# A second routing round held back in the list of the first expert's work, and its steps listed closer together

## The chip, the cores and the metric

The kernel runs on one core of one Trainium2 chip. Its time is the device time of one launch in microseconds (us), the median of several runs. A core has five engines with a queue each, and each queue is worked off in the order in which the program lists it: TensorE (PE, matrix products), VectorE (DVE), ScalarE (ACT), GpSimd (POOL) and SyncE (SP, which here only issues transfers).

## What is computed

The reference chains three blocks over 4608 tokens of width 512. Retention attention makes x. A dense block with 2048 hidden units follows, and then a block of eight experts with 1024 hidden units each, in which every expert gets exactly 576 tokens:

```
x = retention(q, k, v)                    # 4608 x 512
x = (h - tanh(h)) @ w_out,  h = x @ w_in
logits = x @ w_gate                       # 4608 x 8
pairs (token, expert) in falling order of logit: take a pair if the token is
still free and the expert has fewer than 576 tokens
out[tokens of e] = relu(x[tokens of e] @ w1[e]) @ w2[e]
```

Products have single-precision accuracy: each operand is split into a high and a low part, and three products (high-high, high-low, low-high) are added.

## The kernel before

Attention and the dense block take the first 1017 us of the profiled execution and are not touched. What follows is `phase_c`: routing and experts.

**Routing** is done in eight rounds (`route(r)`). A round settles which expert is filled next (`EI[r]`, line 990) and which 576 tokens it gets (`IDX[r]`, line 1050). A round is one long chain that goes to and fro between VectorE and TensorE: proposals (lines 857 to 863, the mask `P`), then six threshold steps, each with a comparison (`cmp`, lines 839, 908, 925), nine or eighteen small matmuls that count (930 or 934), a scaling `ca` (938), small matmuls (949, 950) and a search (957 to 960); then `GG` (969), matmuls 973 and 975, the choice of the expert (979 to 990), matmuls 995 and 996, positions (999 to 1018), `R` on ScalarE (1019), `A` and `R` on VectorE (1021, 1023), matmuls 1027 and 1045, and the list of tokens.

**An expert** (`experts(r)`) runs 192 matmuls of its first layer (line 1158, eight blocks f of 24) and 112 of its second (line 1189, five token tiles in the order 0, 4, 1, 2, 3). After each block of the first layer ScalarE makes `hh` (1167) and a split weight `w2h` (1074), GpSimd makes `w2l` (1075), and VectorE makes the low part `hl` (1171), which is listed six matmuls into the next block. The PSUM pool `psF` has four buffers of which a block takes two, so block f+2 waits until `hl` of block f is made.

**The next expert's needs** are prepared meanwhile: eight weight tiles are loaded by SP (1063) as soon as `EI` is known, split by ScalarE (`w1h`) and GpSimd (`w1l`, both 1074/1075); five token tiles are gathered by GpSimd (`xg`, 1097) from the list of tokens, turned by TensorE (`tp`, 1112, two buffers), copied by ScalarE (`xh`, 1114) and subtracted by VectorE (`xl`, 1115).

**The order in each queue** is set by three generators, `threads`: 0 for routing, 1 for weights, 2 for tokens. Each `yield d` says how many units later the next step may be listed. The expert loop calls `tick` as it lists matmuls (0.24 units for two of the first layer, 0.213 for one of the second); a thread whose time has come lists its next step there. For routing d is scaled by `YS[0]` while only the first round's token list exists and by `YS[1]` after that; for weights and tokens it is scaled by `YS[0]` throughout. No number of these is a time on the chip; they only place instructions.

Before expert 0 the first round runs alone. Then 14 matmuls keep TensorE busy (1215) while the first tokens are gathered, and the second round (r = 1) and the turning of the five token tiles are listed into one another until expert 0 starts. The second round then goes on inside expert 0, the third inside expert 1, and so on; the last two rounds end inside expert 5.

Of the kernel before, what the change touches and what calls it, by code (L numbers as in the profile page):

```python
# [125 lines left out]
@with_exitstack  # L126
def moe_kernel(ctx, tc, qkv, wio, wgt, wgk, ident, w1, w2, qtab, vtab, amask, cint, rtf, rti, rth, rtb, out):
    nc = tc.nc
    ctx.enter_context(tc.manual_schedule())
    cpool = ctx.enter_context(tc.tile_pool(name="cpool", bufs=1))  # L130
    dpool = ctx.enter_context(tc.tile_pool(name="dpool", bufs=1, space=DRAM))
    x2d = dpool.tile([NTOK, DM], F32, name="x2d")
    L = cpool.tile([128, NCOL, E], F32, name="L")

    with ExitStack() as bs:
        phase_ab(tc, bs, qkv, wio, wgt, wgk, ident, qtab, vtab, amask, cint, x2d, L)
    with ExitStack() as cs:
        phase_c(tc, cs, w1, w2, rtf, rti, rth, rtb, x2d, L, out)
# [594 lines left out]

Y_TR, Y_CA, Y_H, Y_GG, Y_X, Y_Z, Y_R, Y_IX = 2.0, 0.85, 0.5, 2.9, 2.7, 4.2, 1.8, 2.7

YS = 0.82, 0.85
TK1 = 0.24
TK2 = 0.213

# [9 lines left out]
def phase_c(tc, ctx, w1, w2, rtf, rti, rth, rtb, x2d, L, out):  # L749
# [369 lines left out]
    def each(f):  # L1119
        for r in range(E):  # L1120
            for d in f(r):
                yield d

    threads = [[0.0, each(f)] for f in (route, weights, tokens)]
    clock = [0.0]

    def tick(dt):
        clock[0] += dt
        for th_ in threads:
            while th_[1] is not None and th_[0] <= clock[0]:  # L1130
# [3 lines left out]
                else:  # L1134
                    th_[0] = clock[0] + d * (YS[len(IDX) > 1] if th_ is threads[0] else YS[0])

# [77 lines left out]
    for _ in range(WARM2):  # L1214
        nc.tensor.matmul(warm, B["ones"], tb[:, 256:768], start=True, stop=True)

    threads[2][0] = 2.0
    while 0 not in XT:
        tick(0.2)
    for r in range(E):  # L1220
# [83 lines left out]
```

## Time and profile before

| | |
|---|---|
| median of 3 runs | 1554.09 us (1553.83 to 1555.44) |
| profiled execution, its own time | 1556.99 us |
| its span, first to last instruction | 1555.1 us |
| TensorE busy | 1456.5 us, 94% of the span |
| VectorE, ScalarE, GpSimd busy | 73%, 49%, 36% |
| mean granted TensorE clock | 0.973 of full speed |
| expert 0, first matmul | 1070.40 us into the span |

Times in the rows below are us from the span's start. The profiled execution has 1.9 us around its span, and lies 2.9 us above the median of the runs; differences are worked out within its span and then put on the median.

### The profile page before, as it was taken

The numbers are of one execution on the slowest core, as the hardware profiler recorded it, in microseconds if no ns is written. First come the engines' busy times: TensorE is split into PE (matmuls) and PEld (weight loads), VectorE is DVE, ScalarE is ACT, GpSimd is POOL, SyncE is SP. The second block draws the span as 40 slices with busy tenths as digits, with TensorE's granted clock in tenths as the row PEclk, the third lists the DMA queues.
The fourth block names the chain that finished last, engine by engine and source line by source line (L and its number), as shares of the span: only waits on it lengthen the run. The fifth ranks groups of instructions, "written<-read, shape, count | busy, mean of one in ns | idle before, by whom it ended". The sixth has DMA issues, their size and how long they took to land.

```text
span 1555.1 us, 26174 instructions
## 1 busy us (share of the span) xinstructions
PE 1456.5 (94%) x9500; PEld 1276.3 (82%) x9500; DVE 1132.7 (73%) x2740; ACT 761.5 (49%) x1585; POOL 558.3 (36%) x492
## 2 busy tenths in 40 slices
PE   5989899899999999999999999937999999999997
PEld 4777788789898989898989898825788887887996
DVE  7999965878787878777878787867776766765210
ACT  4767775455656565656564646503333323323421
POOL 4546541212222221212121223224535535446541
PEclk7999999999999999999999999967999999999999
DMA  7522222111111111111111100013423423426210
GB/s 258 197 72 82 82 104 74 43 62 42 62 41 62 42 62 42 62 41 62 42 54 50 43 22 21 1 37 129 125 85 124 129 85 120 130 84 193 91 65 31
DMA packets 48610, 122.43 MB, mean 79 GB/s; under 512 B 6624, under 2 KB 13408, under 8 KB 48224
## 3 DMA queue, kind: packets, MB, share of 16 engines
q1 hardware_dynamic: 41184, 99.80, 19.2%
q0 software_dynamic: 6144, 19.93, 4.0%
q8 instruction: 75, 1.23, 0.3%
q10 hardware_dynamic: 1152, 1.02, 0.2%
q14 instruction: 55, 0.45, 0.1%
HBM read 101.85 MB, written 18.87 MB: 78 GB/s over the span
## 4 chain that ended last, share of the span: by engine, by line
PE 73%; DVE 14%; issue 4%; ACT 3%; POOL 2%; DMA 1%; SPq 0%; POOLq 0%; DVEq 0%; ACTq 0%
PE h L426 22%; PE x L489 21%; PE ff L1189 11%; PE ff L1158 10%; PE pb L290 2%; PE pb L357 2%; PE pb L369 1%; DVE work L208 1%; DVE t L456 1%; DVE t L450 1%; DVE junk L530 1%; DVE t L452 1%; PE tp L1112 1%; PE pb L305 1%; DVE h L454 1%
## 5 line engine op out<-in xcount | busy, mean ns | idle before, releaser
L470 POOL TENSOR_TENSOR gl<-t,gh 128x384 fp32r<-128x384 f32 x192 | 200.2, 1043 | 652.6 <-ACT gh L467 565.8
L426 PE MATMUL h<-xh,w0h 128*128 128x384 f32 x704 | 240.4, 341 | 11.8 <-DVE t L456 11.6
L426 PE MATMUL h<-xh,w0l 128*128 128x384 f32 x704 | 238.3, 338 | 0.0
L436 ACT ACTIVATE S<-h 128x384 f32<-128x384 f32 x192 | 93.7, 488 | 286.7 <-PE h L426 286.5
L489 PE MATMUL x<-w1h,gh 128*128 128x512 f32 x576 | 231.2, 401 | 0.5 <-ACT gh L467 0.5
L489 PE MATMUL x<-w1l,gh 128*128 128x512 f32 x576 | 226.9, 394 | 0.0
L489 PE MATMUL x<-w1h,gl 128*128 128x512 f32 x576 | 217.0, 395 | 1.3 <-POOL gl L470 1.0
L450 DVE SCALAR_TENSOR_TENSOR t<-t,S 128x384 f32<-128x384 f32 x192 | 114.1, 594 | 128.7 <-ACT t L439 128.1
L530 DVE SCALAR_TENSOR_TENSOR junk<-x2r,wg 128x512 f32<-128x512 f32 x240 | 168.7, 703 | 5.2
L426 PE MATMUL h<-xl,w0h 128*128 128x384 f32 x704 | 152.6, 338 | 0.0
L426 PEld LDWEIGHTS h<-xh,w0h 128*128 128x128 f32 x704 | 132.7, 188 | 23.4 <-DVE t L456 12.3
L1075 POOL TENSOR_TENSOR w2l<-ws,w2h 128x512 fp32r<-128x512 f32 x64 | 82.6, 1293 | 161.4 <-ACT w2h L1074 161.4
L426 PEld LDWEIGHTS h<-xh,w0l 128*128 128x128 f32 x704 | 133.1, 189 | 6.7
L489 PEld LDWEIGHTS x<-w1h,gl 128*128 128x128 f32 x576 | 108.1, 188 | 29.7 <-POOL gl L470 5.7
L1189 PE MATMUL ff<-w2h,hh 128*128 128x512 f32 x320 | 127.5, 399 | 3.1 <-DVE hl L1171 2.0
L456 DVE COPY_PREDICATED t<-m,h 128x384 f32<-128x384 uint16 x192 | 114.4, 596 | 20.9 <-ACT m L445 1.7
L1189 PE MATMUL ff<-w2l,hh 128*128 128x512 f32 (+1 forms) x320 | 127.4, 398 | 0.6 <-POOL w2l L1075 0.6
L489 PEld LDWEIGHTS x<-w1h,gh 128*128 128x128 f32 x576 | 108.6, 188 | 22.9 <-ACT gh L467 1.3
L426 PEld LDWEIGHTS h<-xl,w0h 128*128 128x128 f32 x704 | 126.7, 189 | 0.3 <-DVE xl L413 0.2
L439 ACT ACTIVATE t<-S,bias 128x384 f32<-128x384 f32 x192 | 118.3, 616 | 17.4 <-POOL gl L470 0.9
L489 PEld LDWEIGHTS x<-w1l,gh 128*128 128x128 f32 x576 | 108.6, 189 | 17.1
L1158 PE MATMUL ff<-xh,w1h 128*128 128x288 f32 x512 | 115.0, 302 | 6.3 <-DVE hl L1171 5.5
(212 smaller groups left out, 2989.6 us busy)
## 6 DMA issues: line engine op xcount, KB each, us to landing
ws<-in_w SPq DMA_DIRECT2D x128, 256.0 KB, 2.8
ain<-in_qkv SPq DMA_DIRECT2D x36, 768.0 KB, 4.2
wst<-in_wio SPq DMA_DIRECT2D x32, 512.0 KB, 3.5
x2d<-x2r SPq DMA_DIRECT2D x33, 256.0 KB, 2.0
w1h<-in_qkv SPq DMA_DIRECT2D x12, 192.0 KB, 4.6
w1l<-in_qkv SPq DMA_DIRECT2D x12, 192.0 KB, 3.5
w0h<-in_qkv SPq DMA_DIRECT2D x12, 192.0 KB, 4.0
w0l<-in_qkv SPq DMA_DIRECT2D x12, 192.0 KB, 4.1
```

Of the source, the lines that this page charges most:

```text
L290: nc.tensor.matmul(PSA[k][a][:, chunk(c)], kt[r, chunk(c)], q[r, chunk(c)], start=True, stop=True)
L426: nc.tensor.matmul(h[:, :TB], w[0][f][:, hp, :], x, start=i == 0, stop=i == 11)
L436: nc.scalar.activation(S, h, AF.Square, scale=KSC)
L439: nc.scalar.activation(AT[s][2], AT[s][1], AF.Square, bias=bias[:, 0:1])
L450: nc.vector.scalar_tensor_tensor(t, t, PA - PB * PB / 4, S, op0=OP.add, op1=OP.mult)
L456: nc.vector.copy_predicated(t, m.bitcast(U16), h)
L470: nc.gpsimd.tensor_tensor(G[s][1], TT.pop(s), G[s][0].bitcast(F32), op=OP.subtract)
L489: nc.tensor.matmul(X2[n][i], g[:, i * 128:i * 128 + 128], w, start=(f == 0 and g is gh and w is wh), stop=(f == NF - 1 and g is gl))
L530: nc.vector.scalar_tensor_tensor(j, r, 1.0, wg[e // 4][:, e % 4, :], op0=OP.mult, op1=OP.mult, accum_out=L[:, c, e:e + 1])
L1075: nc.gpsimd.tensor_tensor(l, s, h.bitcast(F32), op=OP.subtract)
L1158: nc.tensor.matmul(ps[u], w[:, k, :], x[:, k, 288 * u:288 * u + 288], start=i == 0, stop=i == 11)
L1189: nc.tensor.matmul(o, h, w, start=f == 0 and i == 0, stop=f == 7 and i == len(prods) - 1, skip_group_check=t == 4)
```

## The change

Two places change. The scale of the second routing round, and of all later steps of weights and tokens, goes from 0.82 to 0.75. And after the warm-up matmuls the first four steps of the second round are listed at once (its proposals on VectorE, as before), and its next step may be listed only from 7.0 units on, while the tokens' thread still starts at 2.0.

```
-YS = 0.82, 0.85
+YS = 0.75, 0.85
@@ phase_c, after the warm-up matmuls (line 1215)
-    threads[2][0] = 2.0
+    for _ in range(4):
+        next(threads[0][1])
+    threads[0][0], threads[2][0] = 7.0, 2.0
     while 0 not in XT:
         tick(0.2)
```

What this does to the queues at three places follows.

VectorE ahead of expert 0. `ca`, `cmp` and the rows from 957 on are the second round's; `xl` are the five token tiles of expert 0. Before:

```order
L938 TENSOR_TENSOR ca<-rt,tf 128x32
L1115 TENSOR_TENSOR xl_10796<-tp,xh_10795 128x4x128
L957 TENSOR_REDUCE d_10822<-rt 128x8
L958 TENSOR_REDUCE dm_10819<-d_10822 128x1
L959 STREAM_TRANSPOSE tr_10820<-dm_10819 128x32
L960 SCALAR_TENSOR_TENSOR tr_10820,pi<-tr_10820,st 128x31
L916 TENSOR_SCALAR st<-tf,pi 128x32
L925 TENSOR_TENSOR cmp_10827<-hi,st 128x1152
L1115 TENSOR_TENSOR xl_10796<-tp,xh_10795 128x4x128 x2
L938 TENSOR_TENSOR ca<-rt,tf 128x32
```

After:

```order
L1115 TENSOR_TENSOR xl_10796<-tp,xh_10795 128x4x128 x4
L938 TENSOR_TENSOR ca<-rt,tf 128x32
L1115 TENSOR_TENSOR xl_10796<-tp,xh_10795 128x4x64
L957 TENSOR_REDUCE d_10850<-rt 128x8
L958 TENSOR_REDUCE dm_10847<-d_10850 128x1
L959 STREAM_TRANSPOSE tr_10848<-dm_10847 128x32
L960 SCALAR_TENSOR_TENSOR tr_10848,pi<-tr_10848,st 128x31
L916 TENSOR_SCALAR st<-tf,pi 128x32
L925 TENSOR_TENSOR cmp_10855<-hi,st 128x1152
```

All five token tiles now stand ahead of the round's next search and comparison; the matmuls 930 that wait for that comparison move from between the third and fourth tile to behind 16 matmuls of expert 0.

ScalarE at the end of expert 0's first layer: the last block's `hh` and `w2h`, the routing's `R`, and the first split weights `w1h` of expert 1. Before:

```order
L1074 ACTIVATE w2h_11286<-ws_11121 128x512
L1019 ACTIVATE R<-b_11382,tf 128x36x20
L1167 ACTIVATE hh<-ff 128x288 x2
L1074 ACTIVATE w2h_11390<-ws_11177 128x512
L1074 ACTIVATE w1h_11399<-ws 128x512
```

After:

```order
L1074 ACTIVATE w2h_11270<-ws_11095 128x512
L1167 ACTIVATE hh<-ff 128x288 x2
L1074 ACTIVATE w2h_11323<-ws_11148 128x512
L1074 ACTIVATE w1h_11379<-ws 128x512
L1074 ACTIVATE w1h_11389<-ws 128x512
L1019 ACTIVATE R<-b_11416,tf 128x36x20
```

`R`, which waits for a long chain on VectorE, stood ahead of the last block's `hh` and now stands behind it and behind two split weights. On GpSimd, at the same place, the first gather for expert 1 stood behind seven of the eight `w1l` and now stands behind all eight.

TensorE at the end of expert 1's first layer; 995 and 996 are the third round's. Before (18 first-layer matmuls still follow these rows):

```order
L1158 MATMUL ff<-xh_11583,w1h_11517 128x288 x2
L995 LDWEIGHTS tb
L995 MATMUL rt<-X,tb 128x72
L996 LDWEIGHTS tb
L996 MATMUL rt<-X,tb 128x72
L1158 MATMUL ff<-xh_11583,w1l_11518 128x288 x2
```

After:

```order
L1158 MATMUL ff<-xl_11577,w1h_11502 128x288 x8
L995 LDWEIGHTS tb
L995 MATMUL rt<-X,tb 128x72
L996 LDWEIGHTS tb
L996 MATMUL rt<-X,tb 128x72
L1189 MATMUL ff<-w2h_11772,hh 128x512
```

The routing steps stand some 18 matmuls later within expert 1, and 995 is now the last thing ahead of the second layer, the place at which it stood in expert 0 before.

## Rows read from the trace of the kernel before

**Rows 1.** The page: engines' busy time (share) xinstructions, and the weight loads
```profile
PE 1456.5 (94%) x9500; PEld 1276.3 (82%) x9500; DVE 1132.7 (73%) x2740; ACT 761.5 (49%) x1585; POOL 558.3 (36%) x492
...
ws<-in_w SPq DMA_DIRECT2D x128, 256.0 KB, 2.8
```

**Rows 2.** Timeline, start of expert 0: start, us, engine, line, operation, count [idle before <-releaser]
```profile
1065.00 0.69 DVE L1115 TENSOR_TENSOR xl<-tp,xh 128x512 fp32r<-128x512 f32 x1 [1.15 <-ACT xh L1114]
1065.71 0.19 DVE L957 TENSOR_REDUCE d<-rt 128x8 f32<-128x32 f32 x1
...
1065.75 0.66 PE L1112 MATMUL tp<-tf,xg 128*128 128x128 f32 x4 [1.11 <-DVE xl L1115]
1065.77 1.26 ACT L1114 ACTIVATE xh<-tp 128x512 fp32r<-128x512 f32 x2 [0.81 <-PE tp L1112]
...
1066.90 1.35 DVE L925 TENSOR_TENSOR cmp<-hi,st 128x1152 bf16<-128x1152 int32 x1
...
1068.31 0.39 PE L930 MATMUL rt<-P,cmp 128*128 128x32 bf16 x9 [1.91 <-DVE cmp L925]
...
1070.40 0.59 PE L1158 MATMUL ff<-xh,w1h 128*128 128x288 f32 x1
...
1075.19 0.61 PE L934 MATMUL rt<-P,cmp 128*128 128x16 bf16 x18 [0.73 <-DVE cmp L925]
```

**Rows 3.** Windows: us; PE, PEld, DVE, ACT, POOL busy (xinstructions); granted clock, DMA share, GB/s
```profile
1066.00:1068.00 2.00, 0.40 (x4) 0.16 (x2) 1.86 (x6) 0.97 (x2) 2.00 (x3) 1.00 0.27 107
...
1070.00:1072.00 2.00, 2.00 (x11) 2.00 (x10) 1.62 (x7) 0.59 (x2) 2.00 (x2) 0.50 0.00 0
```

**Rows 4.** Timeline, TensorE in expert 0's first layer: two places of the second round
```profile
1081.25 0.39 PE L930 MATMUL rt<-P,cmp 128*128 128x32 bf16 x9
...
1097.81 0.42 PE L973 MATMUL rt<-GG,tb 128*128 128x192 bf16 x3
```

**Rows 5.** Timeline, end of expert 0's first layer: the choice of expert 1, its loads
```profile
1100.06 0.14 DVE L990 TENSOR_SCALAR ei<-mx 128x1 int32<-128x1 f32 x1
...
1101.32 5.15 SPq L1063 DMA_DIRECT2D ws<-in_w  x8
```

**Rows 6.** Timeline, ScalarE and TensorE at expert 0's second layer: R and the waits
```profile
1104.92 0.90 ACT L1019 ACTIVATE R<-b,tf 128x720 bf16<-128x720 bf16 x1 [6.35 <-DVE b L1018]
...
1106.98 0.50 PE L1189 MATMUL ff<-w2h,hh 128*128 128x512 f32 x1 [1.08 <-ACT w2h L1074]
...
1108.35 0.50 PE L1189 MATMUL ff<-w2l,hh 128*128 128x512 f32 x1 [0.63 <-POOL w2l L1075]
...
1123.05 0.66 PE L1112 MATMUL tp<-tf,xg 128*128 128x128 f32 x4 [0.68 <-DMA xg<-x2d,idx]
...
1125.47 0.66 PE L1112 MATMUL tp<-tf,xg 128*128 128x128 f32 x4 [0.36 <-DMA xg<-x2d,idx]
```

**Rows 7.** Timeline, GpSimd there: split weights of expert 1 and the first gather
```profile
1108.25 5.05 POOL L1075 TENSOR_TENSOR w1l<-ws,w1h 128x512 fp32r<-128x512 f32 x4
...
1119.67 0.97 POOL L1097 DMA_INDIRECT xg<-x2d,idx  x1 [0.30 <-DVE lo L903]
```

**Rows 8.** Waits of TensorE, 1140 to 1556 us: line waited for: total, times, longest us
```profile
PE ff L1158 <- DVE hl L1171: 5.5, 6, 2.0
PE ff L1189 <- DVE hl L1171: 2.0, 2, 1.1
PE tp L1112 <- DVE xl L1115: 1.4, 1, 1.4
```

**Rows 9.** Timeline, TensorE: the longest waits of experts 1, 3, 4 and 5
```profile
1165.62 0.50 PE L1189 MATMUL ff<-w2h,hh 128*128 128x512 f32 x1 [1.10 <-DVE hl L1171]
...
1285.96 0.89 PE L1158 MATMUL ff<-xh,w1h 128*128 128x288 f32 x2 [1.99 <-DVE hl L1171]
...
1342.67 0.89 PE L1158 MATMUL ff<-xh,w1h 128*128 128x288 f32 x2 [1.10 <-DVE hl L1171]
...
1402.81 0.89 PE L1158 MATMUL ff<-xh,w1h 128*128 128x288 f32 x2 [1.20 <-DVE hl L1171]
```

## Prediction, made before the changed kernel was run

> **What bounds the kernel now.** I read the page first. TensorE is busy for 1456.5 us of the 1555.1 us span, 94%, VectorE for 1132.7, the other two for far less [rows 1]. The change takes away no matmul and adds none, so the time can move in two ways only: TensorE's idle time at waits, and the clock at which it runs. The second view is the timeline at the start of expert 0, where the list is changed [rows 2, 3]; the reader is to see there which wait ends last before each matmul. The third is the end of expert 0, where every routing step now stands later than before [rows 4 to 7]. The fourth is the list of TensorE's waits over the later experts [rows 8, 9], since the new scale acts on all of them.
>
> At the start the turning of expert 0's tokens and the search of the second round share VectorE and TensorE. The fourth tile's `tp` waits 1.11 us for `xl`, which came behind earlier work of the round, and the nine matmuls 930 wait 1.91 us for `cmp`, with the last turn behind them [rows 2]. TensorE is busy for 0.40 us of the 2 us from 1066; its granted clock is 1.00 there, and 0.50 (1.2 GHz) from 1070 to 1072, when expert 0's matmuls have begun [rows 3].
>
> In the late experts TensorE waits mostly for `hl`: 5.5 us ahead of first-layer matmuls, 2.0 ahead of second-layer ones, plus 1.4 for one `xl` [rows 8]. Together that is 8.9 us, the largest part of what a new order can win or lose behind expert 0.
>
> **Start of expert 0.** With the round held back, `tp` depends on ScalarE and VectorE's token copies alone. Two `xh` take 1.26 us, so one takes 0.63, and one `xl` takes 0.69 [rows 2]. With two `tp` buffers the last tiles follow each other at about 1.3 us: third tile at about 1065.5, fourth 1066.8, the last (half a tile) 1068.1, and its `xl` is done by about 1068.8. `ca` follows at once. Expert 0's first matmul then comes at about 1069.0 instead of 1070.40: **1.4 us won** (1.1 to 2.1).
>
> What was held back is paid for next. The chain from 957 to the end of `cmp` runs from 1065.71 to 1066.90 + 1.35, that is 2.54 us [rows 2]. It now starts when `ca` and the last `xl` are done, about 0.8 us behind the first matmul, so `cmp` is ready 3.3 us behind it. 930 stands behind 16 matmuls; at full clock they take 16 x 0.135 = 2.2 us (112 of them with the small matmuls between take 1097.81 - 1081.25 = 16.56 us, 0.148 each [rows 4]; without the small ones I put one at 0.135). So 930 waits about 1.1 us. The next step, 934, stands 42 matmuls later (6.0 us with what lies between), and its chain of `ca`, search and two `cmp` takes about 6.7, so it waits 0.7; before it waited 0.73 [rows 2], which is no change. Low clock: the window 1070 to 1072 at half speed cost about 1.0 us [rows 3]. With shorter idle times ahead I take it as gone at this place. First matmul 1069.0, plus 60 x 0.135, plus the two waits, plus 0.9 for the small matmuls is 1079.9. Before, 930 behind 60 matmuls ran at 1081.25 [rows 4]. So **-1.35 us** after a third of the first layer (bounds -2.1, if both waits are absent, and 0, if both chains are one us longer than read).
>
> **End of expert 0.** Here the new scale does more than the hold. 973 ran behind 172 first-layer matmuls [rows 4] and now stands four matmuls into the second layer; 995 goes from the end of the first layer to 14 matmuls into the second.
>
> What goes: `R` stood ahead of the last `hh` on ScalarE, idle for 6.35 us before it. Because of this `w2h` came 1.08 us late and `w2l` 0.63 [rows 6]. With `R` behind them both waits go: **-1.7 us**.
>
> What comes: VectorE has the last `hl` ahead of the choice of the expert now, so `ei` moves from 1100.06 [rows 5] to about 1103.3. SP issued the loads 1.26 us later [rows 5]; a load takes 2.8 us [rows 1], then one `w1h`. So the first `w1l` starts at about 1107.95, hardly different from 1108.25, because before `R` had held `w1h` back too. GpSimd took 11.4 us from its first `w1l` to the first gather, with seven `w1l` and two stores between [rows 7]. Now all eight stand ahead: 5.05 / 4 = 1.26 more, and the gather starts at about 1120.7. It landed 3.38 us after it started (1119.67 to 1123.05 [rows 6, 7]), so the first turn can run at 1124.2. TensorE gets there earlier than before: the turn stands five second-layer matmuls later (b80 instead of b75), but 1.35 and 1.7 us are saved and one step of the third round has moved behind it. I work out 1120.0. So it **waits 4.2 us** where it waited 0.68 + 0.36 [rows 6]: +3.2. The other four gathers follow in 1.26 us each, the turns every 1.6, so they don't wait. Bounds: nothing, if GpSimd comes to the gather at 1116.6 or before; 5.5, if a store to `out` gets in its way by another us. I take 4.2 because every term has its own row.
>
> Sum up to the end of expert 0: -1.35 - 1.7 + 3.2 = **+0.1**. The gain of the start is spent within one expert.
>
> **Clock behind the new wait.** At the start an idle stretch was followed by 2 us at 0.50, costing 1.0 [rows 3]. A single wait of 4.2 us is longer than the idle time there. Between 0 and 1.0, I take **+0.5**, as nothing shows whether the fall comes while TensorE waits (and costs nothing) or behind it. On this the Trainium skill (TensorE: Matmul & The Clock Gate, section "HAM oscillation — how this bites in real kernels") says that a matmul loop that stops for transfers is throttled again at each stop and begins its next burst at the low clock. By that rule this term would be 1.0 and the forecast 1557.1; it speaks against this change, which trades a wait for VectorE at a place that was slow already for a wait for a gather.
>
> **Later experts.** Every routing step stands some 18 matmuls later in each expert, which is nearly what one expert shifts the round anyway. So expert k+1 of after should look like expert k of before: one more expert of the early, crowded kind. Before, experts 1 to 5 wait for 1.1 (its second layer), about 2.0, 2.6 (of which 1.99 is one wait), 1.1, and 2.6 (of which 1.20): 9.4 us [rows 8, 9]. After: expert 1 gets what expert 0 had, with 995 at the end of its first layer and `R` ahead of the last `hh`: 1.7 [rows 6], plus about 1.1 at a gather that follows; expert 2 some 1.2; expert 3 some 2.1; expert 4 the 2.0 of expert 3 and 1.1 of its own [rows 9]; expert 5 some 2.1. That is 11.3, **+1.9**. Bounds: -4 (most of the `hl` waits go, since `hl` comes to stand ahead of the searches that delay it) and +4 (each of the five experts keeps its wait and the one of its neighbour).
>
> Total: +0.1 + 0.5 + 1.9 = +2.5 us, 1559.5 by the profiled execution's own 1556.99 and 1556.6 on the median, since that execution lies 2.9 above the median. What this kernel's measurement can tell from no change is about 0.2%, 3.1 us: the forecast lies just inside.
>
> **Rivals.** *The `hl` waits go (faster).* One mechanism, in experts 2 to 5 on VectorE: `hl` waits behind a search or comparison listed ahead of it, and with the steps moved by 18 of a block's 24 matmuls it may stand ahead of them. It decides at whether VectorE can begin `hl` when `hh` is ready; if so the 7.5 us of [rows 8] shrink to 3 to 4. For it: that is the largest group of waits. Against it: the same move puts other `hl` behind other steps, as in experts 3 to 5 of before. Price: later experts -3 instead of +1.9, so about 1551.6. *All late steps lose (slower).* The gather wait costs 5, the clock a full 1.0, 1027 waits for an `R` that stands behind two `w1h`, and the later experts lose 4: +6, about 1559.8. For it: the gather stands behind all eight `w1l` on a queue of one. Against it: nothing shows that waits at neighbouring experts add. *Nothing happens.* The start's 1.4 us are eaten by 930 and 934, the turn's wait is some 2 us shorter than worked out because GpSimd's order is looser than read, and the later waits only change place: about 1554.
>
> **How the numbers follow.** Forecast 0.48, centre 1556.6, its own range 1555 to 1558.3; `hl` waits go 0.13; all lose 0.26; nothing 0.13. Slower by over 0.2% (above 1557.2) takes the second rival whole and 0.15 of the forecast: 0.41. Faster by over 0.2% (below 1551.0) takes most of the first: 0.12. Within: 0.47. The range of 1552.5 to 1560.0 leaves out about 0.1 at either end.
>
> **What would show it.** First matmul of expert 0 at about 1069.0; a wait of about 1.1 us at 930 behind 16 matmuls. No wait for `w2h` or `w2l` in expert 0, and waits of 1.08 and 0.63 us of this kind at expert 1 instead. The first gather at about 1120.7 and the first turn behind it with a wait of about 4.2 us for `xg`: this is the step on which most hangs, and if that turn doesn't wait, the forecast is 3 to 4 us too high. The granted clock behind that wait at 0.50. The wait list from 1140 on with about 11 us for `hl`, `w2h`, `xg` and `xl`; if it holds 5, the first rival was right.

## The result and the profile after

| | before | after |
|---|---|---|
| median | 1555.11 us (6 runs) | 1564.52 us (1562.27 to 1566.95, 6 runs) |
| ratio, 95% interval | | 1.006 (1.0047 to 1.0074) |
| profiled execution's span | 1555.1 us | 1565.2 us |
| TensorE busy | 1456.5 us | 1464.3 us |
| mean granted clock | 0.973 | 0.968 |

The change costs 9.4 us; 2.5 had been forecast, with 1560.0 as the upper end. TensorE runs the same 9500 matmuls and is busy for 7.8 us more: a part of that is matmuls that ran at a lower clock.

The start did what the prediction said. Timeline of TensorE after, then the windows there (columns as in [rows 2, 3]):

```profile
1067.49 0.59 PE L1158 MATMUL ff<-xh,w1h 128*128 128x288 f32 x1
...
1070.89 0.39 PE L930 MATMUL rt<-P,cmp 128*128 128x32 bf16 x9
```

```profile
1066.00:1068.00 2.00, 1.53 (x14) 1.18 (x11) 1.10 (x4) 0.94 (x2) 2.00 (x3) 0.69 0.00 0
1068.00:1070.00 2.00, 2.00 (x10) 2.00 (x9) 1.83 (x8) 0.00 (x0) 2.00 (x3) 0.50 0.00 0
```

Expert 0's start is counted from matmul 995 of the first round, before and after:

```profile
1049.39 0.24 PE L995 MATMUL rt<-X,tb 128*128 128x72 bf16 x1 [1.95 <-DVE ei L990]
...
1048.00 0.24 PE L995 MATMUL rt<-X,tb 128*128 128x72 bf16 x1 [1.95 <-DVE ei L990]
```

It starts 19.49 us behind it instead of 21.01: 1.52 us won. What follows, from the first matmul of an expert to that of the next (both profiled executions, us):

| expert | before | after | difference | what lies in it after |
|---|---|---|---|---|
| 0 | 65.45 | 67.81 | +2.36 | 1045 waits 3.14, clock behind it costs 3.42; gone are 1.71 and 1.04 of [rows 6] |
| 1 | 60.27 | 66.28 | +6.01 | `hl` three times, `w2h` and `w2l` 1.60, gathers 1.00 |
| 2 | 61.36 | 61.75 | +0.39 | |
| 3 | 62.94 | 60.50 | -2.44 | the 1.99 of [rows 9] is gone |
| 4 | 59.83 | 65.27 | +5.44 | `hl` 2.23 and two smaller, clock 1.71 |
| 5 | 61.14 | 61.19 | +0.05 | `xl` 2.15 |
| 6 | 53.22 | 54.35 | +1.13 | one gather 0.95 |

They sum to +12.94. Less the 1.52 of the start, and less 1.39 by which the untouched part ahead was shorter in this execution, that is the difference of the spans, 10.1. The table holds one execution of each kernel; that of the changed one was its slowest, 2.4 us above its median.

The end of expert 0, where `R` jammed ScalarE before. Timeline after, of several engines:

```profile
1106.75 0.90 DVE L1023 TENSOR_TENSOR R<-b,st 128x720 bf16<-128x720 bf16 x1
...
1108.86 0.78 PE L1027 MATMUL rt<-R,A 128*128 128x160 bf16 x9 [0.47 <-ACT R L1019]
...
1110.53 1.66 ACT L1074 ACTIVATE w1h<-ws 128x512 fp32r<-128x512 f32 x3
...
1112.21 0.59 ACT L1196 ACTIVATE o<-ff 64x512 f32<-64x512 f32 x1
...
1112.84 0.68 DVE L1197 TENSOR_TENSOR o<-ff,o 64x512 f32<-64x512 f32 x1 [5.19 <-ACT o L1196]
1113.45 0.18 DVE L1031 TENSOR_TENSOR st<-st,vd 128x36 f32<-128x36 f32 x1
...
1114.66 0.43 DVE L1040 TENSOR_REDUCE ix<-im 128x40 bf16<-128x160 f32 x1
...
1115.15 0.27 PE L1045 MATMUL rt<-ix,tb 128*128 128x10 bf16 x4 [3.14 <-DVE ix L1040]
...
1119.42 0.98 POOL L1097 DMA_INDIRECT xg<-x2d,idx  x1 [0.16 <-DVE m L861]
```

VectorE has nothing to do for 5.19 us, since the addition for expert 0's half tile (1197) stands at its head and waits for ScalarE's copy 1196. That copy stands behind seven split weights of expert 1, the last of which end at 1112.19. Lines 1031 to 1040 stand behind the addition, though the matmuls 1027 that they need were issued at 1108.86, and 1045 waits for them. Before, 1027 was listed at 30 of the second layer's 112 matmuls, ahead of the half tile's store at 40; now it is at 41, behind it. The timeline before shows the other order; 1197 waited there too, but nothing that TensorE needed soon stood behind it:

```profile
1111.27 0.46 DVE L1040 TENSOR_REDUCE ix<-im 128x40 bf16<-128x160 f32 x1
...
1113.30 0.26 PE L1045 MATMUL rt<-ix,tb 128*128 128x10 bf16 x4
...
1113.90 0.68 DVE L1197 TENSOR_TENSOR o<-ff,o 64x512 f32<-64x512 f32 x1 [2.17 <-ACT o L1196]
```

The windows after show the clock at this wait and behind it (the column ahead of the last two):

```profile
1112.00:1114.00 2.00, 0.01 (x1) 0.00 (x0) 1.09 (x5) 1.30 (x3) 1.86 (x2) 1.00 0.78 298
1114.00:1116.00 2.00, 0.85 (x6) 0.76 (x7) 1.90 (x8) 0.00 (x0) 2.00 (x3) 0.63 0.19 72
1116.00:1118.00 2.00, 2.00 (x7) 1.52 (x6) 1.90 (x5) 0.00 (x0) 1.81 (x3) 0.50 0.00 0
1118.00:1120.00 2.00, 2.00 (x6) 1.61 (x5) 1.90 (x6) 0.00 (x0) 1.84 (x2) 0.50 0.30 66
1120.00:1122.00 2.00, 2.00 (x7) 1.54 (x7) 0.45 (x4) 0.60 (x1) 1.39 (x3) 0.66 0.44 102
1122.00:1124.00 2.00, 2.00 (x19) 1.50 (x18) 0.00 (x0) 0.00 (x0) 1.70 (x2) 1.00 0.72 180
```

Busy with second-layer matmuls all the time, TensorE starts one of them every 0.43 us at clock 0.50 (at 1118.41, 1118.84, 1119.26), and one every 0.23 from 1121.38 on. The part of the clock that is missing between 1114 and 1122 sums to 3.42 us. The wait and the clock behind it thus come to 6.6 us at one place of the list. That is not the net loss there: older waits went, and expert 0 as a whole is 2.36 us longer. The larger part of the 12.94, 10.58, lies in experts 1 to 6.

The later experts. TensorE's waits from 1140 on, which answer to [rows 8]:

```profile
PE ff L1158 <- DVE hl L1171: 5.9, 8, 2.2
PE tp L1112 <- DMA xg<-x2d,idx: 2.9, 5, 0.9
PE tp L1112 <- DVE xl L1115: 2.2, 1, 2.2
PE ff L1189 <- DVE hl L1171: 1.2, 1, 1.2
PE rt L1027 <- DVE R L1023: 1.0, 1, 1.0
PE ff L1189 <- ACT w2h L1074: 1.0, 1, 1.0
```

And the timeline at two of them, in expert 1's second layer and in expert 4's first:

```profile
1171.44 0.90 ACT L1019 ACTIVATE R<-b,tf 128x720 bf16<-128x720 bf16 x1 [7.35 <-DVE b L1018]
...
1173.50 0.50 PE L1189 MATMUL ff<-w2h,hh 128*128 128x512 f32 x1 [0.96 <-ACT w2h L1074]
...
1351.33 0.89 ACT L1019 ACTIVATE R<-b,tf 128x720 bf16<-128x720 bf16 x1 [7.36 <-DVE b L1018]
...
1353.07 1.10 PE L1158 MATMUL ff<-xh,w1h 128*128 128x288 f32 x2 [2.23 <-DVE hl L1171]
```

In both, ScalarE stands idle over 7 us for `R`, with a finished block's `hh` behind it: the picture of [rows 6], once an expert later, and once more where the wait bears the name of `hl`. Before, these two places were in experts 0 (1.71 us) and 3 (the 1.99 of [rows 9]); now they are in experts 1 (1.60) and 4 (2.23). The waits at `R` have moved by one expert and have hardly grown.

### The profile page after: what moved, and what is told of

It is laid out like the page before. It is cut to its first block, busy times and chain, and to the rows that moved or that the text cites. A ratio compares the mean times of both kernels' runs of the same rounds, so it can differ in the third digit from the quotient of the medians.

```text
span 1565.2 us, 26175 instructions
## 1 busy us (share of the span) xinstructions
PE 1464.3 (94%) x9500; PEld 1280.7 (82%) x9500; DVE 1131.7 (72%) x2740; ACT 761.7 (49%) x1585; POOL 558.3 (36%) x492
```

## The experiments

Each ratio below is to the kernel before, run beside it on the same chip. That kernel's median was 1556.36 us beside the first four experiments, 1552.68 beside the next four and 1556.15 beside the last three, so ratios are compared, and times only within such a group. The expectations call the addition 1197 a subtraction.

**The two parts apart.** The hold alone is the changed kernel with `YS = 0.82, 0.85`; the scale alone is the kernel before with `YS = 0.75, 0.85`.

> The hold alone: the second round still stops until four tiles are turned, but the scale stays 0.82. Theory A (the loss sits at one place, the end of expert 0: the store's subtraction 1197 stands on VectorE ahead of 1031 to 1040, so that 1045 waits 3.1 us, and the clock falls behind it for 3.4): 1045 stands at b59 instead of b51 here, so its wait shrinks from 3.1 to 1.5 us or less, the clock may hold, and the time is 3 to 6 us below the changed kernel's 1564.5, about 1560. Theory B (every routing step that stands later costs, in every expert): here the steps of expert 0 stand later still, so the time is 1565 or more, and the waits of experts 1 to 5 sum to over 12 us.

> The scale alone: 0.75, no hold, so that every step stands earlier than in either kernel (995 behind 180 matmuls of expert 0's first layer, 1045 at b31). Theory A: 1031 to 1040 stand ahead of the subtraction of the store, no wait at 1045, clock at 1.00 through expert 0's second layer; the start is as before (first matmul at about 1070.4); 1553 to 1557. Theory B: earlier steps cost less, so it is faster than the kernel before, about 1550. If it is slower than 1560, neither is right and the scale itself is what costs.

Hold alone: 1.0036 (1.0023 to 1.0048). Scale alone: 1.0006 (0.9996 to 1.0016). The hold costs, the scale by itself costs nothing that can be told. Theory A's price for the hold, about 1560, came out (1.0036 of 1555.11 is 1560.7), but not for its reason. The wait did not shrink with 1045 listed later; it came at 1027, since the same addition 1197 now stood ahead of 1023 (timeline, hold alone):

```profile
1111.90 0.68 DVE L1197 TENSOR_TENSOR o<-ff,o 64x512 f32<-64x512 f32 x1 [4.37 <-ACT o L1196]
1112.51 0.89 DVE L1023 TENSOR_TENSOR R<-b,st 128x720 bf16<-128x720 bf16 x1
...
1113.45 0.80 PE L1027 MATMUL rt<-R,A 128*128 128x160 bf16 x9 [3.42 <-DVE R L1023]
```

But against theory B the later experts of the hold alone wait less than those of both parts together (`hl` ahead of the first layer: 3.0 us from 1140 on, against 5.9), and all waits of its experts 1 to 5 sum to 9.5 us, where theory B wanted over 12: later is not simply worse. Nor is earlier better: by its ratio the scale alone is at 1556, in theory A's range, where theory B wanted 1550.

**The end of expert 0.** In the changed kernel the addition and store of expert 0's half tile are listed two matmuls later, behind 1040:

```
+                    if late and t == 1 and 3 * f + i == 2:
+                        late.pop()()
...
-                V.tensor_tensor(o[:n], ps[:n], o[:n], op=OP.add)
...
+            if t == 4 and r == 0:
+                late.append(store)
...
```

> The changed kernel, with the store of expert 0's half tile (subtraction on VectorE and its transfer) listed two matmuls later, behind 1040; nothing else moves. Theory A: the wait of 3.1 us at 1045 goes, and the fall of the clock right behind it. GpSimd's first gather doesn't move (about 1119.4), so TensorE reaches the first turn some 6.5 us earlier, at about 1118.6, and waits about 4 us there for xg: the wait that the prediction named and that the other one had covered. Net 0 to 3 us below 1564.5. If no wait for xg comes: 6.5 below, 1558. Rival: the subtraction isn't what holds 1031, then nothing changes.

```profile
1116.77 0.98 POOL L1097 DMA_INDIRECT xg<-x2d,idx  x1 [0.16 <-issue]
...
1120.17 1.11 PE L1112 MATMUL tp<-tf,xg 128*128 128x128 f32 x4 [2.77 <-DMA xg<-x2d,idx]
```

1045 no longer waits; instead the first turn waits 2.77 us for its gather, with the clock low for 1.70 behind it. 1.0038 (1.0023 to 1.0052). The wait for the gather that the prediction named had been covered by the one ahead of it. That cover is shown by this run. The gain, about 3 us by the ratios, is not: this interval and the changed kernel's overlap, and in the profiled executions expert 0 is only 0.95 us shorter (66.86 for 67.81).

With the last three split weights of expert 1 listed behind the gathers as well (`GD[1]` is set behind the fifth):

```
+            while r == 1 and f == 5 and not GD.get(r):
+                yield 0.3
             split_w(r, 1, f)
```

> As the run with the store moved, and the last three split weights of expert 1 (ScalarE and GpSimd) are listed behind the five gathers. Theory A with the covered wait: both waits go, the clock stays at 1.00 through expert 0's second layer, first gather at about 1113; some 6.5 us below the changed kernel, 1558, which is still above the 1555.1 of before, as experts 1 to 5 keep their own waits (some 15 us with the pair behind each). If the time stays at 1562 or above, the end of expert 0 is not where the loss is.

In the profiled execution (2.5 us faster than this run's median) the turn waits 1.13 us and no clock is lost in expert 0, which takes 63.51 us, less than before the change (65.45). But the time is 1.0039 (1.0029 to 1.0049): no better than with the store alone, some 3 us better than unrepaired, with intervals that just touch. Some 6 us of the loss are still there, so they lie behind expert 0.

**`R` on ScalarE.** The step 1019 is put off until a block's `hh` and `w2h` are listed, or, where no block ends in time, to just ahead of `A` (1021):

```
-        nc.scalar.activation(R[:, :, 1, :], b1, AF.Copy, scale=F["p"])
+        RL.append(lambda: nc.scalar.activation(R[:, :, 1, :], b1, AF.Copy, scale=F["p"]))
         yield Y_Z
+        while RL:
+            RL.pop()()
...
             split_w(r, 2, f)
+            while RL:
+                RL.pop()()
...
```

> The run with store and gathers moved, and R on ScalarE (1019) always listed behind the next block's hh and w2h instead of ahead of them. Theory C (R, which waits some 3 to 6 us for VectorE, holds up the hh that stands behind it; which expert is hit depends on where the 18 matmuls of shift put 995 against the block ends: 0 and 3 before, 1 and 4 now): the waits for w2h and w2l at expert 1 (0.96 + 0.63) and the wait for hl of 2.15 + 0.46 at expert 4 go, together 4.2 us; 1027 may wait up to 1 us more at one place. Against the run without it about -3.5, to some 1559. If the wait at expert 4 stays, it is VectorE's own queue and not R.

> The kernel before with that one move of R. Theory C: the waits for w2h and w2l at expert 0 (1.08 + 0.63) and the one of 1.99 + 0.46 at expert 3 go, -4.1 us, about 1552, faster than the kernel before. Rival (the cover idea): where R is late no longer, the turn at expert 0 waits for its gather longer by what was saved (xg 0.68 becomes 2.4), and only expert 3's 2.4 is won: about 1554.

On top of the last kernel: 0.9994 (0.9984 to 1.0004), 7 us less than without it where 3.5 were expected, although inside expert 0 the move itself did harm, since it brought `R` behind five split weights, and 1027 waited 3.35 us. On the kernel before: **0.9954 (0.9938 to 0.9971)**, 6.6 us, more than the 4.1 of theory C; the rival, that the turn at expert 0 waits longer by what was saved, did not come (its two waits sum to 1.58 us, 1.04 before). Its waits of TensorE from 1140 on:

```profile
PE ff L1161 <- DVE hl L1174: 2.9, 5, 1.1
PE ff L1194 <- DVE hl L1174: 1.1, 1, 1.1
PE rt L930 <- DVE P L863: 0.2, 1, 0.2
```

The 1.99 at expert 3 became 0.65. And a wait that I had not put down to `R` went too, the 1.42 us for `xl` of [rows 8] in expert 5: there `R` had stood ahead of the token copy `xh`. Experts 0, 2, 3 and 5 are shorter by 1.96, 1.39, 1.38 and 2.92 us, the others as before.

**Where the steps stand.** From the kernel with store and gathers moved, the scale of the third round is 0.80 as long as that round is inside expert 1. From expert 2 on every step of the routing then stands within 4 matmuls of its place in the kernel before (the token turns stand up to 10 earlier):

```
-                    th_[0] = clock[0] + d * (YS[len(IDX) > 1] if th_ is threads[0] else YS[0])
+                    th_[0] = clock[0] + d * ((YS[len(IDX) > 1] if len(IDX) != 2 else 0.8) if th_ is threads[0] else YS[0])
```

> The run with store and gathers moved, and the third round's scale 0.80 instead of 0.85 for as long as it is inside expert 1, so that from expert 2 on every step stands within 4 matmuls of where the kernel before has it. Theory D (where the steps stand against the block ends is what the later experts cost, not the hold): waits of experts 1 to 5 fall from 17.5 to about 12 as in the kernel before, and the time by 4 to 6 us against the run without it, to 1557. Rival (the crowding stays whatever the position): no change, 1562.

> All four moves: store, gathers, R, and the third round's scale. If C and D add: 1562 - 3.5 - 5, some 1553 to 1554, and with 1.5 us won at the start the first version with the hold that isn't slower than the kernel before. If they repair the same waits: 1557.

1.0008 (0.9998 to 1.0017), and with `R` behind `hh` 0.9958 (0.9943 to 0.9973), by this ratio some 1549 us, less than either number expected. One constant that shifts later experts by some 14 matmuls gives back 0.3%, with the hold still in place, and with `R` moved in both it gives back as much (0.9994 to 0.9958). Expert 1 goes from 66.72 us to 63.25 and expert 4 from 63.73 to 59.98; TensorE's waits in experts 1 to 5 fall from 13.8 us to 9.3, as few as in the kernel before (9.4). The longest groups of them from 1140 on, without the shift and then with it:

```profile
PE ff L1161 <- DVE hl L1174: 4.9, 7, 2.1
PE tp L1115 <- DVE xl L1118: 2.9, 2, 2.1
PE tp L1115 <- DMA xg<-x2d,idx: 1.7, 4, 0.6
...
PE ff L1161 <- DVE hl L1174: 3.2, 4, 1.6
PE tp L1115 <- DVE xl L1118: 2.1, 1, 2.1
...
PE tp L1115 <- DMA xg<-x2d,idx: 0.9, 2, 0.5
```

So the later experts pay for where the steps stand, and not for the hold as such. That it is the place against the block ends which counts, as theory D says, is argued: only this one shift was tried. With both moves the gains add, though in expert 0 1027 again waits 3.37 us.

**The parts put together.** `R` put off only from the third round on, and beside it again the kernel before with `R` behind `hh`, and the changed kernel with that one move:

```
+        if r == 1:
+            RL.pop()()
```

> All four moves, but the second round's R (inside expert 0) listed at once, as in the changed kernel: there it stands among the split weights of expert 1, and putting it off made 1027 wait 3.37 us. Theory (that wait is a fault of the move and nothing else): 1027 waits some 0.55 again, and with a gather wait of about 1 us the net is -2 to -3 against the version without this, about 0.993 of the kernel before, the fastest of all. If the turn waits for its gather in place of it, no change.

> The kernel before with R behind hh, beside the version with the hold on the same chip. If the hold's earlier start (about 1 us) reaches the end once the places behind it are repaired, this one is 1 to 2 us slower than the other; if both are equal, the hold is worth nothing even then.

> The changed kernel with R behind hh from the third round on, and nothing else. Theory C: w2h and w2l at expert 1 (0.96 + 0.63) and most of the wait of 2.23 + 0.46 at expert 4 go, with the fall of the clock behind that where it comes; the wait of 3.14 at 1045 and the clock behind it stay. So -4 to -6 us of the changed kernel's +9.4: 1.002 to 1.0035 of the kernel before.

| kernel | ratio to before | 95% interval |
|---|---|---|
| changed kernel, all four moves, `R` only from the third round on | 0.9934 | 0.9922 to 0.9946 |
| before, `R` behind `hh` | 0.9949 | 0.9936 to 0.9962 |
| changed kernel, `R` behind `hh` from the third round on | 1.0013 | 1.0005 to 1.0022 |

The first is the fastest of all, 1545.31 us beside 1556.15, as expected, and 1027 waits 0.41 us. Its waits from 1140 on:

```profile
PE ff L1166 <- DVE hl L1179: 1.5, 3, 0.6
PE tp L1120 <- DVE xl L1123: 0.6, 1, 0.6
PE tp L1120 <- DMA xg<-x2d,idx: 0.3, 1, 0.3
```

It is 2.2 us faster than the second, which has neither hold nor the other moves, but the intervals overlap. In the profiled executions experts 0 to 6 take the same (416.57 and 416.76 us), and the way from 995 to expert 0's first matmul is 1.91 us shorter in the first. So it is likely that the hold's earlier start reaches the end there; it is not shown, as store, gathers and the shift of one round differ too.

The third leaves the wait at 1045 (3.4 us in its profile) and the low clock behind it in place; its ratio is lower by 0.005 than the changed kernel's 1.006, some 7 us where 4 to 6 were expected. But the same move is worth 0.0046 and 0.0051 on the kernel before. With `R` behind `hh` in both kernels (in the changed one from the third round on) the changed one is still slower by 0.67%, 1557.92 to 1547.51 us on one chip. So what `R` costs, some 0.5%, is paid by both kernels, at different experts, and is no part of the loss as far as these runs can tell. The loss has two other parts. With the end of expert 0 repaired it falls from 0.6% to 0.39%, and with the third round shifted back to 0.08% (0.9998 to 1.0017), with `R` left where it was. For the second step the intervals lie apart, for the first they just overlap.

## Why the prediction was wrong, point by point

**Up to expert 1 the sum came out, by luck.** Start, end of expert 0 and clock were to come to +0.1 + 0.5. Measured, from 995 to the first matmul of expert 1, they came to -1.52 + 2.36 = +0.84, though the terms were others than forecast, as the next three points say. The step that failed in the total is the last one, the later experts.

**The start was right, with two errors that cancelled.** The first matmul came at 1067.49; by its distance from 995 that is 1.52 us won, where 1.4 was said. 930 was to wait 1.1 us and didn't: the clock, which I took as recovered, was at 0.50 until 1070, so the 16 matmuls ahead of 930 took as long as its chain. 934, which was to wait 0.7, didn't either. The low clock cost 1.3 there, the two waits nothing. Behind 60 matmuls the kernel is 1.3 us ahead; the prediction had 1.35.

**The end of expert 0: right queue, incomplete.** `R` no longer jams the last `hh`; `ei` is 2.9 us later as counted from 995 (3.2 said); the first gather is 1.1 us later (1.0 said). What failed is the step "TensorE gets there earlier than before ... 1120.0". I followed GpSimd's queue to the gather, but not VectorE's between 1027 and 1045. The row was there to be seen: in the order, the half tile's addition passes from behind 1040 to ahead of 1031. A moved step has to be followed past every instruction that another engine holds up. In place of the 4.2 us at the turn came 6.6 at 1045 and behind it; the turn then found its gather landed. With the store moved, TensorE stood at the turn at 1120.9, counted from 995 as above (1120.0 said), and waited 2.77.

**The clock term was mis-sized.** I gave it 0.5, between 0 and 1.0, by the start of expert 0. It was 3.42 in expert 0's second layer, behind another wait than the one I had in mind, and 1.71 once more in expert 4. The Trainium skill's rule that I quoted (TensorE: Matmul & The Clock Gate, section "HAM oscillation — how this bites in real kernels") says that each stop makes the next burst begin at the low clock; the stops that it describes are waits for transfers of some 3 to 5 us. The traces agree at 3.14 us here, show the same behind a shorter stop, 2.77 with the store moved, and don't agree at 3.37 in the run with all four moves, behind which the clock stayed at 1.00.

**The later experts: the step that failed.** From "expert k+1 of after should look like expert k of before" I took +1.9, with bounds of -4 and +4. It was +10.6 (experts 1 to 6 in the table of the result). As to `R` the sentence held: the jam of [rows 6] came again at expert 1 (0.96 and 0.64 us, 1.7 said), the 1.99 of expert 3 at expert 4 (2.23). What failed is the price that I put on standing some 18 matmuls later for everything else:

- TensorE's waits rose by 5.3 us, from 9.4 to 14.7, not by 1.9. The gathers took 2.9 of it, in experts 1, 2 and 6, where I had put one wait of 1.1. The first layer of expert 1 has three waits for `hl`, 2.0 together, behind searches and comparisons on VectorE, where it had none before.
- The clock fell in expert 4: 1.71.
- Some 3.6 us stand in no wait row. A part is that a wait for `hl` costs more than its row says: a pair of first-layer matmuls that has waited for `hl` takes 0.89 us instead of 0.43. But there are eight such pairs now (one of them at the low clock) and were six before, so this is 0.9 at most; the rest I can't place.

What the runs showed in its place is that the position of the steps is the cost: the one shift of the third round took the waits of experts 1 to 5 from 13.8 us back to 9.3 and the ratio from 1.0039 to 1.0008. In the timeline after, the first of the three waits for `hl` in expert 1, with the comparison that stands ahead of `hl` and an ordinary pair:

```profile
1141.05 0.43 PE L1158 MATMUL ff<-xh,w1l 128*128 128x288 f32 x2
...
1141.64 1.35 DVE L839 TENSOR_TENSOR cmp<-lf,st 128x1152 bf16<-128x1152 f32 x1
1142.91 0.75 DVE L1171 SCALAR_TENSOR_TENSOR hl<-ff,hh 128x288 fp32r<-128x288 f32 x2
...
1143.41 0.89 PE L1158 MATMUL ff<-xh,w1h 128*128 128x288 f32 x2 [0.88 <-DVE hl L1171]
```

**The rivals.** The slow one, with 1559.8, had the right sign and named the clock and the neighbouring experts, which lost; the gather and 1027, which it named too, were not where expert 0 lost. Its price was too small, and its own +6 on 1554.1 is 1560.1, not 1559.8, so that it lay outside the stated range.

## What to carry to other kernels

When a change shifts instructions in a list, walk each engine's queue past everything that moved and ask of each neighbour what holds *it* up. An instruction that waits long for another engine, such as `R` here, belongs behind the work that is ready, but not behind too much of it: the move was worth 0.46% on the kernel before and as much on the changed one, and did harm where it put `R` behind five split weights. Before a gain like this is called the repair of a loss, the same move has to be tried on the kernel that hasn't the loss. And when a wait is repaired and nothing is won, look for the next wait that it had covered.

## What the runs showed of the hardware

The price of one and the same wait differs between executions by what the clock does behind it. The wait of 2.23 us at expert 4 was followed by 1.71 us lost to a lower clock; in the run with the store moved, the same wait, 2.17 us, was followed by none. The wait of 2.15 us for `xl` in expert 5 was followed by none in the changed kernel, and by 1.71 in the run with the gathers moved. Of the waits in expert 0's second layer, 3.14 us (changed kernel) and 3.40 (the same with `R` moved) were followed by 3.4 us, 3.42 (hold alone) and 3.35 (store, gathers and `R` moved) by 1.71, and 3.37 (all four moves) by none. In none of the profiled executions was a wait under 1.3 us in the later experts followed by a fall.

This goes with the spread of the times. Every execution has its mean granted clock beside its time: the changed kernel's three shortest (1562.27 to 1563.16 us) were at 0.971 to 0.975, the three longest (1565.88 to 1566.95) at 0.968 to 0.969. The 21 executions of the kernel before beside the first experiments spread as wide (5.0 us) and go with the clock too, with a correlation of -0.76.
